# Moving the third pair's AV run behind the last score tile of a batch, in a fused attention and MLP kernel

## The chip, the cores and the metric

One core of one Trainium2 chip. The time is that of the whole program on the device in microseconds, as the median of several executions. A profiled execution also has a span, from the first to the last instruction, about 2 us shorter than the time, and a granted TensorE clock, 1.0 being full speed. A ratio of two kernels is the record's, made from their fast runs in the same rounds on the same chip; it isn't quite the ratio of the medians quoted beside it. All runs here count as fast but one of the kernel before (346.41 us at a clock of 0.985, beside e1 to e4), which the ratios leave out; where other runs had a slightly lower clock, that is said.

## The reference, cut to what matters

```python
scores = q @ k.T / 8 + (cum[:, None] - cum[None, :])   # cum: running sum of log f; causal
attn   = softmax(scores)
x      = attn @ v                   # 8 batches x 8 heads, 576 x 64
out    = gelu(x @ w_in) @ w_out     # 4608 x 512 -> 2048 -> 512
```

## The kernel before

Heads go in four pairs. A pair's scores are four tiles in PSUM, the memory that TensorE writes to, each of both heads: the two heads' matmuls contract over 64 rows and run side by side on the two halves of the array. ScalarE takes the exp of a tile, GpSimd masks the diagonal, and the AV run (the exps times v, 15 matmuls a head, contracting over all 128 rows) follows one pair later. VectorE divides by the row sums, a DMA transposes the result, and gemm1 reads it. Between the tiles stand steps of the previous batch's gemm2: "r" is a pair of half-array matmuls (contracting 64 rows each, into two banks that VectorE adds), "n" one full-array matmul. "r" steps go between scores because both use half-array mode.

```python
s_psum = tile_pool("s_psum", bufs=2)   # score tiles, two banks each   (abbreviated)
o_psum = tile_pool("o_psum", bufs=2)   # AV accumulators, one a head
m_psum = tile_pool("m_psum", bufs=2)   # gemm banks
...
PLAN = [                                # gemm2 steps of the previous batch
    (0, "o", 16 * "r"),
    (1, "m", 6 * "r" + "n" + 8 * "r" + "n"),
    (2, "m", 9 * "r" + "n" + 6 * "r"),
    (3, "s", 5 * "r" + 11 * "n"),
]
FILL = [[7, 6, 3, 3], [1, 3, 3, 2], [1, 3, 3, 3], [1, 3, 3, 3], [5]]
...
for i in range(HP):                     # 4 head pairs
    for t in range(4):
        scores(b, i, t)
        take(fill, counts[i][t])        # so many gemm2 steps
        if i and t == 1:
            av(i - 1)                   # AV and normalize of both heads
            x_dma(b, i - 1)
        ...
take(fill, counts[HP][0])
av(HP - 1)
x_dma(b, HP - 1)
take(fill, 4)
...
take(fill, 999)
# then gemm1 of this batch
```

Batch 0 and 1 have code of their own, which isn't changed. Batch 2 has its own lists, since it carries more gemm2 work; batches 3 to 7 use the lists above. In the profile L299 is a score matmul, L330 an AV matmul, L479 a gemm2 step, L385 gemm1, L309 the exp, L311 the mask, L343 and L344 the division, L487 and L490 the copy of one gemm2 bank and the addition of the other. PE stands for TensorE's matmuls, PEld for its weight loads, ACT for ScalarE, DVE for VectorE and POOL for GpSimd. A line of a timeline has start and length in us, engine, source line and operation, and in brackets the engine's idle time before it and what ended that.

The softmax here doesn't subtract the row's maximum and nothing guards it: scores larger than these inputs give would overflow.

## Time and profile before

| | before |
|---|---|
| median of 3 runs | 343.51 us (342.83 to 344.71) |
| profiled execution | 341.0 us, span 339.1 us, clock 0.998 |
| TensorE busy | 96% of the span, 90% of the chain that ended last |
| batch 3, 4 or 5, first score tile to the next batch's | 35.39 us |
| of it the fourth pair's first tile to the first gemm1 matmul | 8.69 us |
| the same stretch in batch 2 | 11.54 us |

The views behind this table are in the prediction, batch 2's with the result. The chain follows the work that ended last back, at each step to what it had waited for. The views are read as follows: TensorE is full, so only gaps in its stream and its own work can be won; a wait of another engine matters only where TensorE waits for it in turn.

### The profile page before, as it was taken

Reading aid. Unit: us, or ns where it says so; the run is one execution under the profiler, and the core shown is the slowest. Engines: PE = TensorE matmul, PEld = TensorE weight load, DVE = VectorE, ACT = ScalarE, POOL = GpSimd, SP = SyncE. Lnnn points to the kernel's source line nnn. Section 1 sums busy time; section 2 is a strip of 40 time slices with the busy share of each in tenths; the row PEclk is TensorE's granted clock in tenths of the full one; section 3 lists DMA queues with packets and bytes.
Section 4 is the critical chain, followed back from the end, with each engine's and each line's share of the span. In section 5 each row is a group of like instructions: output and inputs, shape, how many; then the busy total and the mean of one; then the engine's idle time right before and its main releaser. Section 6 shows DMA issues by size and latency. Waiting matters only on the chain.

```text
span 339.1 us, 7794 instructions
## 1 busy us (share of the span) xinstructions
PE 325.5 (96%) x3129; PEld 171.6 (51%) x3170; DVE 184.3 (54%) x417; ACT 209.9 (62%) x299; POOL 121.5 (36%) x250
## 2 busy tenths in 40 slices
PE   8799899999999999999999999999999999999995
PEld 4574455445554456445644565446544654444443
DVE  4770446664358935895579646974696541020011
ACT  6977786773735787378737873787368755404600
POOL 8190395037437053713453343624351420000000
PEclk9999999999999999999999999999999999999999
DMA  7999999979999799299959598589900241011013
GB/s 118 180 167 192 210 186 143 194 143 188 209 172 181 116 205 189 83 139 130 223 132 138 112 198 177 77 137 208 173 31 2 82 80 44 0 63 64 0 38 88
DMA packets 104628, 44.18 MB, mean 130 GB/s; under 512 B 83408, under 2 KB 100048, under 8 KB 104592
## 3 DMA queue, kind: packets, MB, share of 16 engines
q1 hardware_dynamic: 87296, 29.52, 45.4%
q0 software_dynamic: 16896, 13.63, 27.1%
q8 instruction: 25, 0.41, 0.5%
q10 hardware_dynamic: 400, 0.52, 0.4%
q14 instruction: 11, 0.09, 0.1%
HBM read 36.85 MB, written 9.44 MB: 137 GB/s over the span
## 4 chain that ended last, share of the span: by engine, by line
PE 90%; issue 2%; DMA 2%; ACT 2%; POOL 1%; DVE 1%; SPq 0%; POOLq 0%; DVEq 0%; ACTq 0%
PE ps L385 36%; PE ps L479 26%; PE o L330 10%; PE ps L421 8%; PE s L299 7%; DMA v_sb<-in_v_dram 2%; PE ps L517 2%; ACT e L309 1%; PE ps_x L363 1%; POOL q L107 1%; SPq L119 0%; POOL k L107 0%; PE ps_f L207 0%; DVE x L344 0%; DVE vw L268 0%
## 5 line engine op out<-in xcount | busy, mean ns | idle before, releaser
L405 ACT ACTIVATE g<-ps 128x512 bf16<-128x512 f32 x144 | 82.1, 601 | 80.3 <-PE ps L385 80.3
L309 ACT ACTIVATE e<-s 128x896 bf16<-128x896 f32 (+2 forms) x128 | 100.8, 834 | 26.6 <-PE s L299 24.5
L385 PE MATMUL ps<-xT,w_in_sb 128*128 128x512 bf16 x502 | 111.8, 379 | 0.5
L479 PE MATMUL ps<-w_out_sb,g 64*128 64x512 bf16 (+1 forms) x712 | 101.9, 376 | 0.8 <-issue 0.5
L385 PEld LDWEIGHTS <-w_in_sb 128*128 128x128 bf16 x576 | 55.9, 98 | 67.6 <-issue 1.8
L311 POOL TENSOR_SCALAR_AFFINE_SELECT e<-e 128x256 bf16<-128x256 bf16 (+1 forms) x135 | 49.1, 383 | 93.6 <-ACT e L309 93.3
L479 PEld LDWEIGHTS <-g 64*128 64x128 bf16 (+1 forms) x736 | 41.9, 94 | 39.8 <-issue 9.0
L299 PE MATMUL s<-qT,kT 64*128 64x320 bf16 (+4 forms) x384 | 45.6, 276 | 3.5 <-ACT e L309 2.3
L268 POOL TENSOR_TENSOR vw<-v_sb,wT 128x640 bf16<-128x640 f32 x30 | 38.6, 1289 | 24.9 <-PE s L299 14.5
L249 DVE COPY qT<-tq 64x288 bf16<-64x288 bf16 x96 | 42.2, 440 | 3.4 <-DMA tq<-q 2.0
L249 DVE COPY kT<-tk 64x288 bf16<-64x288 bf16 x96 | 40.7, 424 | 2.4 <-DMA tk<-k 0.8
L487 DVE COPY ot<-ps 128x512 f32<-128x512 f32 x25 | 17.3, 692 | 41.8 <-PE ps L479 41.8
L330 PE MATMUL o<-vw,e 128*128 128x65 bf16 x960 | 36.6, 194 | 3.0 <-issue 2.4
L330 PEld LDWEIGHTS <-e 128*128 128x128 bf16 x960 | 34.1, 98 | 6.8 <-POOL e L311 2.5
L344 DVE TENSOR_TENSOR x<-o,r 128x320 bf16<-128x320 f32 x64 | 31.5, 492 | 2.4 <-DMA xT<-x 0.2
L430 DVE COPY ot<-ps 128x512 f32<-128x512 f32 (+2 forms) x9 | 5.7, 632 | 48.9 <-PE ps L421 46.1
L299 PEld LDWEIGHTS <-kT 64*128 64x128 bf16 x384 | 19.7, 94 | 24.3 <-issue 11.7
L421 PE MATMUL ps<-w_out_sb,g 128*128 128x512 bf16 (+2 forms) x142 | 27.9, 355 | 0.1
L343 DVE RECIPROCAL r<-o 128x5 f32<-128x5 f32 x64 | 12.1, 190 | 22.9 <-PE o L330 22.7
L421 PEld LDWEIGHTS <-g 128*128 128x128 bf16 x144 | 13.5, 98 | 14.5
L490 DVE TENSOR_TENSOR ot<-ot,ps 128x512 f32<-128x512 f32 x25 | 17.2, 687 | 1.4
L385 PE MATMUL ps<-tails,w_in_sb 128*128 128x512 bf16 x62 | 14.2, 377 | 0.2
(67 smaller groups left out, 133.6 us busy)
## 6 DMA issues: line engine op xcount, KB each, us to landing
out_dram<-ot SPq DMA_DIRECT2D x32, 256.0 KB, 2.6
v_sb<-in_v_dram SPq DMA_DIRECT2D x24, 256.0 KB, 4.8
q<-in_q_dram POOLq DMA_DIRECT2D x6, 576.0 KB, 6.3
k<-in_k_dram POOLq DMA_DIRECT2D x6, 576.0 KB, 8.3
v_sb<-in_v_dram SPq DMA_DIRECT2D x22, 128.0 KB, 4.9
w_in_sb<-in_moe_w_in_dram POOLq DMA_DIRECT2D x4, 512.0 KB, 7.9
w_out_sb<-in_moe_w_out_dram POOLq DMA_DIRECT2D x4, 512.0 KB, 9.0
q<-in_q_dram POOLq DMA_DIRECT2D x4, 144.0 KB, 4.4
```

Of the source, the lines that this page charges most:

```text
L249: nc.vector.tensor_copy(rows[:, odd], src[odd * D : (odd + 1) * D, 2 * i + h].rearrange("d j p -> d p j"),)
L268: eng.tensor_tensor(vw(b)[:, hs, :, 0:D], v_sb[:, hs, :, :], w.unsqueeze(3).to_broadcast([P, 2, NBLK, D]), Alu.mult,)
L299: nc.tensor.matmul(to, *ab, start=half < 0, stop=half == 1 or not masked)
L309: nc.scalar.activation(et[:, :, z:c], st[:, :, z:c], Act.Exp, scale=scale)
L311: nc.gpsimd.affine_select(out=et[:, :, c0 + z : c0 + P], in_=et[:, :, c0 + z : c0 + P], compare_op=Alu.is_ge, fill=0.0, base=z, pattern=[[ ...
L330: nc.tensor.matmul(o[:, m, :], e_of[b, i, t][:, h, c : c + P], vw_of[b][:, 2 * i + h, n, :], start=(n == 0), stop=(n == m),)
L344: nc.vector.tensor_tensor(x_of[b, i][:, :, h, :], o[:, :, 0:D], r.unsqueeze(2).to_broadcast([P, NBLK, D]), Alu.mult,)
L385: nc.tensor.matmul(ps, w_in_sb[:, kt, ffb * P : (ffb + 1) * P], src[:, kt, 0:TC], start=(kt == 0), stop=(kt == n_dm - 1),)
L405: nc.scalar.activation(g_of[c][ffb], ps, Act.Gelu)
L421: nc.tensor.matmul(pss[ts][:, c0:c1], g_of[c][kt][:, ts * P : (ts + 1) * P], w_out_sb[:, kt, c0:c1], start=(kt == 0), stop=(kt == n_ff - 1),)
L479: nc.tensor.matmul(banks[r], g_of[c][kt][rows, ts * P : (ts + 1) * P], w_out_sb[rows, kt, :], start=kt == (steps.index("r") if r else 0), ...
L487: nc.vector.tensor_copy(ot, banks[1])
```

## The change

The intent: the third pair's AV run leaves its place between the fourth pair's second and third tile, where it costs a switch from half-array to full-array mode and one back, and goes behind the last tile, next to the fourth pair's AV run. Full-array gemm2 steps stand between the two runs and between the fourth pair's heads. The number of steps and the row blocks in which they are half- or full-array are fitted to that.

```diff
     PLAN = [ ...
-        (2, "m", 9 * "r" + "n" + 6 * "r"),
-        (3, "s", 5 * "r" + 11 * "n"),
+        (2, "m", 14 * "r" + 2 * "n"),
+        (3, "s", 16 * "n"),
     PLAN_1 = [ ...                        # batch 2
-        (2, "m", 12 * "r" + 4 * "n"),
+        (2, "m", 16 * "n"),
-    FILL = [[7, 6, 3, 3], [1, 3, 3, 2], [1, 3, 3, 3], [1, 3, 3, 3], [5]]
-    FILL_2 = [[8, 8, 8, 8], [8, 8, 4, 4], [4, 4, 4, 4], [4, 4, 4, 4], [4]]
+    FILL = [[7, 6, 3, 3], [1, 3, 3, 2], [1, 3, 3, 3], [2, 2, 2, 2]]
+    FILL_2 = [[8, 8, 8, 8], [8, 8, 4, 4], [4, 4, 4, 4], [6, 6, 5, 5]]
...
-        def av(i):
+        def av(i, n=0):
             for h in range(2):
                 attend(b, i, h, (0, 1, 2, 3, 4))
                 normalize(b, i, h)
+                if h == 0:
+                    take(fill, n)
+            x_dma(b, i)
...
-                if i and t == 1:
+                if i in (1, 2) and t == 1:
                     av(i - 1)
-                    x_dma(b, i - 1)
...
-        take(fill, counts[HP][0])
-        av(HP - 1)
-        x_dma(b, HP - 1)
+        av(HP - 2)
+        take(fill, 2)
+        av(HP - 1, 1)
         take(fill, 4)
```

## The prediction

> **What bounds the kernel now.** I read the busy table first: the share of the span in which TensorE has a matmul running, and the 40 slices, which show it near full from end to end at a granted clock of 1.0. Then the chain that ended last.
>
> ```profile
> PE 325.5 (96%) x3129; PEld 171.6 (51%) x3170; DVE 184.3 (54%) x417; ACT 209.9 (62%) x299; POOL 121.5 (36%) x250
> ...
> PE 90%; issue 2%; DMA 2%; ACT 2%; POOL 1%; DVE 1%; SPq 0%; POOLq 0%; DVEq 0%; ACTq 0%
> ```
>
> TensorE alone sets the time; 90% of the chain is its own work. So a change helps only by what it removes from TensorE's stream: work, switching gaps, or waits. Next I cut one steady batch (the one from 151.73 us) into scores of the first three head pairs, the fourth pair up to the first gemm1 matmul, and gemm1, with the view of busy time by window.
>
> ```profile
> 151.73:164.53 12.80, 12.47 (x169) 7.31 (x172) 7.94 (x21) 10.83 (x14) 4.83 (x14) 1.00 0.99 147
> 164.53:173.22 8.69, 8.48 (x114) 5.00 (x113) 3.94 (x10) 4.90 (x6) 3.90 (x9) 1.00 1.00 208
> 173.22:187.12 13.90, 13.85 (x64) 6.17 (x63) 13.29 (x26) 8.42 (x15) 6.47 (x9) 1.00 0.70 116
> ```
>
> Columns: length, then PE, PEld, DVE, ACT, POOL busy. A batch lasts 35.39 us. In the first stretch ACT is busy 10.83 of 12.80 us: behind TensorE it is a close second in the scores. The change leaves the order up to 164.53 alone, so the middle row is the one that it acts on. TensorE's timeline shows that stretch's skeleton (fourth pair's score tiles at 164.53, 165.07, 167.08 and 167.93; AV runs at 166.03 and 169.88; full-array gemm2 from 171.06):
>
> ```profile
> 165.07 0.37 PE L299 MATMUL s<-qT,kT 64*128 64x64 bf16 x4
> 165.23 0.64 PE L479 MATMUL ps<-w_out_sb,g 64*128 64x512 bf16 x4
> 166.03 1.12 PE L330 MATMUL o<-vw,e 128*128 128x65 bf16 x30 [0.16 <-issue]
> 167.08 0.36 PE L299 MATMUL s<-qT,kT 64*128 64x448 bf16 x2
> 167.28 0.81 PE L479 MATMUL ps<-w_out_sb,g 64*128 64x512 bf16 x6
> 167.93 0.30 PE L299 MATMUL s<-qT,kT 64*128 64x320 bf16 x2
> 168.06 1.89 PE L479 MATMUL ps<-w_out_sb,g 64*128 64x512 bf16 x16
> 169.88 1.12 PE L330 MATMUL o<-vw,e 128*128 128x65 bf16 x30
> ```
>
> 64*128 is a half-array matmul (two run side by side, one on each half of the rows), 128*128 a full-array one. And ACT's timeline of the same stretch:
>
> ```profile
> 163.37 1.65 ACT L309 ACTIVATE e<-s 128x896 bf16<-128x896 f32 x2 [0.93 <-PE s L299]
> 165.18 1.62 ACT L309 ACTIVATE e<-s 128x896 bf16<-128x896 f32 x2 [0.16 <-PE s L299]
> 167.54 1.51 ACT L309 ACTIVATE e<-s 128x896 bf16<-128x896 f32 x2 [0.75 <-PE s L299]
> ```
>
> The reader is to see that ACT is idle 0.93 and 0.75 us just after an AV run, and only 0.16 us otherwise: the AV run in the middle of a pair is the time in which the exps catch up.
>
> **What the Trainium skill says.** "TensorEngine Tiling (Array Packing)", Key Properties: changing the tiling mode, not just the tile, drains TensorE. The trace agrees and sizes it. A pair of half-array steps starts every 0.216 us (x16 in 1.89: seven spacings of 0.216 and a last matmul of 0.376). Before the AV at 169.88 the last half-array step started at 169.57, 0.31 earlier: 0.095 more than 0.216. The last AV matmul of the run at 166.03 starts at 166.95 and the scores at 167.08: 0.127, where AV matmuls follow each other at 0.031: 0.096 for the way back. So a switch costs 0.10 us either way. "ScalarE: Activation LUTs", What ACT_TABLE_LOAD costs, gives an ACTIVATE 0.833 ns an element and an overlap of some 93 ns between two; here 896 elements last 0.917 us and follow each other after 0.81, so it agrees, and the trace's values are used.
>
> **The change, part by part.** (a) In batches 3 to 7 the third pair's AV run leaves its place after the fourth pair's second tile and comes after the fourth tile, just before the fourth pair's AV. Before, the stretch has three switches (into AV, back to scores, into AV); after, one: two times 0.10 saved, 0.20 us a batch. The matmul work is equal: 26 gemm2 steps of 0.2155 (half- or full-array alike; the full ones at x10 in 2.32 give the same spacing), two AV runs of 0.95, 1600 score columns in 0.67: 8.2 us of the 8.69.
>
> (b) What the AV run hid comes out. Between the fourth pair's tiles there are now two steps each (0.43 us) and a tile of 0.13 to 0.19 us: about 0.6 a tile, while ACT needs 0.81, 0.71, 0.81, 0.60. Score PSUM has two buffers, so tile 2 waits for the exp of tile 0. Walk, on the half that runs later (0.17 behind, from an earlier wait): its first gemm2 step after tile 0 starts at 164.90, the second at 165.11, tile 1 at 165.33 (0.16), two steps, tile 2 due at 165.92. The exp of tile 0 starts at 165.18 in either kernel and ends 0.92 later, 166.09; a freed buffer is used 0.05 later (the exp that started at 159.37 ended at 160.28, the tile in its buffer started at 160.33): 166.14. Wait 0.22. Tile 3 is due 0.62 later, 166.76; the exp of tile 1 starts 0.81 after the first, 165.99, lasts 0.805: 166.79, and 0.05: 166.85. Wait 0.08. Tile 3 (0.13), two steps (0.43), a switch (0.10): AV of the third pair at 167.51.
>
> (c) The two AV runs are now 0.43 us apart, and the output accumulators have two buffers, one a head. The first head's AV ends about 168.15; VectorE, which has just copied a gemm2 bank (from 167.6, 0.69 us, the next operation 0.60 after its start), does the reciprocal at 168.21 and the scaling from 168.44 for 0.49 us; the buffer is free at 168.98. TensorE wants it at 167.51 + 0.95 + 0.43 = 168.89. Wait 0.10. The second head's buffer is free at about 169.61 and wanted at 168.99 + 0.47 + 0.22 = 169.68: the single step between the heads just covers it. Then 0.47 and 15 full-array steps (3.23): gemm1 starts at 173.38 instead of 173.22. So a batch becomes about 0.17 us longer: -0.20 for the switches, +0.22 +0.08 for ACT, +0.10 for VectorE, less some 0.03 that the old order lost otherwise. Five batches: +0.85.
>
> (d) Batch 2 has its own list. Its third gemm2 row block becomes full-array and begins after the fourth pair's second tile, so scores and full-array steps alternate: five switches where there were three, +0.20. Its first bank is the one that VectorE copies after the last half-array step (0.42 to the copy's start, 0.69, 0.05: free 1.16 after that step's start, wanted at 0.91): +0.25. And +0.05 for the accumulator as in (c). With five or six steps a tile ACT is not in the way. Sum +0.5.
>
> (e) Off the path: one VectorE addition of 0.69 us less a batch, and the transposing DMA of the third pair's output is issued some 2 us earlier or later without effect: the last one lands about 2.6 us after 171.5, and gemm1 asks for it 12 steps after 173.38, at 175.97.
>
> Total +1.35 us: 343.5 becomes 344.9. I lean slightly lower, as the walk counts each wait in full: 344.6.
>
> **Rivals.** First: only the switches count, ACT keeps up. Then five batches give -0.20 each and batch 2 stays within +0.5: 343.0. For it: the idle 0.93 and 0.75 of ACT, which look like slack. Against it: they lie after AV runs, and the waits of TensorE on the exps in the whole trace (2.3 us in 6) show that ACT is already the limit in spots without one. Second: the ACT wait is larger, as the exp of tile 0 may start later, or the masks on GpSimd (0.41 us each, after the exp) reach the fourth pair's AV too late; by the walk they end near 168.7 and are needed at about 169.15. A slip of 0.4 a batch would give 347. Third: the later DMA delays gemm1; its slack of some 1.9 us speaks against it; if it were lost and 0.5 more, the five batches would cost 2.5: 347.
>
> **Range and chances.** The walk's terms are each good to about 0.1 us, together about 0.25 a batch, so 1.3 over five, and the three runs before lie 1.9 apart. Low end 342.7 (the first rival and luck), high end 346.4. All rivals stay far inside 2% (6.9 us): faster 1%, within 2% 97%, slower 2%.
>
> **What would show it right or wrong.** Right: in the changed trace no AV run between the fourth pair's tiles; ACT without idle from that pair's first exp to its last; the third tile about 0.2 us after its two steps would let it start, with the exp named as releaser; the stretch to gemm1 8.85 us against 8.69; and in batch 2 a gap at the first full-array step of the third block. Wrong: ACT idle there, or the stretch at 8.5 or less, as the first rival has it; a wait on GpSimd before the last AV, or on a DMA in gemm1, for the others.

## The result, and the profile after

| | before | after |
|---|---|---|
| first comparison, 6 runs each | 343.17 us (342.60 to 344.71) | 342.92 us (342.66 to 343.23) |
| ratio | | 0.9987, 95% interval 0.9964 to 1.001 |
| span of the profiled execution | 339.1 us | 340.9 us |
| batch 3, 4 or 5 | 35.39 us | 35.74, 35.66, 35.66 us |
| batch 2 | 45.79 us | 46.39 us |

By the times the kernels are the same, with a ratio whose interval has 1 in it. By the two traces the changed kernel is 1.8 us longer, and every batch from 2 on is. (Of batch 3's 35.74 us, 0.09 are a wait for a DMA in gemm1; see (e) below.) The two readings don't fit, and the experiments below begin with that.

The view of busy time by window, after, with the same three stretches of the same batch as in the prediction (columns as there):

```profile
152.65:165.45 12.80, 12.79 (x171) 7.32 (x172) 7.17 (x18) 10.84 (x14) 4.85 (x14) 1.00 0.85 171
165.45:174.40 8.95, 8.88 (x110) 5.13 (x106) 3.65 (x10) 4.79 (x6) 3.91 (x9) 1.00 0.99 175
174.40:188.31 13.91, 13.91 (x66) 6.14 (x65) 13.29 (x28) 8.42 (x15) 6.52 (x9) 1.00 0.68 112
```

The scores of the first three pairs (12.80 us) and gemm1 (13.91 against 13.90) are what they were. The middle stretch, on which alone the change acts, went from 8.69 to 8.95 us. TensorE's timeline of it, after:

```profile
166.41 0.59 PE L479 MATMUL ps<-w_out_sb,g 64*128 64x512 bf16 x3
167.06 0.37 PE L299 MATMUL s<-qT,kT 64*128 64x448 bf16 x2
167.25 0.61 PE L479 MATMUL ps<-w_out_sb,g 64*128 64x512 bf16 x4
167.76 0.31 PE L299 MATMUL s<-qT,kT 64*128 64x320 bf16 x2
167.89 0.61 PE L479 MATMUL ps<-w_out_sb,g 64*128 64x512 bf16 x4
168.43 1.13 PE L330 MATMUL o<-vw,e 128*128 128x65 bf16 x30
169.40 0.59 PE L479 MATMUL ps<-w_out_sb,g 128*128 128x512 bf16 x2
170.00 0.63 PE L330 MATMUL o<-vw,e 128*128 128x65 bf16 x15
170.47 0.38 PE L479 MATMUL ps<-w_out_sb,g 128*128 128x512 bf16 x1
170.69 0.64 PE L330 MATMUL o<-vw,e 128*128 128x65 bf16 x15
```

No AV run stands between the score tiles any more. The third tile starts at 167.06, 1.61 us after the first at 165.45. ScalarE's timeline and one piece of the chain of waits say why:

```profile
166.09 3.02 ACT L309 ACTIVATE e<-s 128x896 bf16<-128x896 f32 x4 [0.16 <-PE s L299]
```

```profile
166.09 0.93 ACT e L309
```

The pair's four exps now run without any pause, where before there was one of 0.75 us after the second. The first of them ends at 167.01, and the third tile, which needs its buffer, starts 0.05 later. The chain of the kernel before has no exp in this stretch; this one runs through it. The second wait is in front of the fourth pair's AV run. Two full-array steps start at 169.40 and 169.61, so the run is due at 169.83; it starts at 170.00. All engines' timeline there, with VectorE's copy and reciprocal just ahead:

```profile
168.54 0.69 DVE L487 COPY ot<-ps 128x512 f32<-128x512 f32 x1 [3.15 <-PE ps L479]
169.15 0.18 DVE L343 RECIPROCAL r<-o 128x5 f32<-128x5 f32 x1
169.37 0.49 DVE L344 TENSOR_TENSOR x<-o,r 128x320 bf16<-128x320 f32 x1
```

```profile
169.97 0.22 PEld L330 LDWEIGHTS <-e 128*128 128x128 bf16 x5 [0.48 <-POOL e L311]
```

The scaling that frees the accumulator ends at 169.86. The weight load follows at 169.97 and the matmul at 170.00. The view names GpSimd's mask as the releaser of that load, but GpSimd's own timeline has its last mask from 169.18 for 0.41 us, so it was done by 169.59; VectorE came last.

In batch 2 the stretch went from 11.54 to 12.14 us. The same view, before and after:

```profile
90.89:102.43 11.54, 11.33 (x130) 6.20 (x129) 5.11 (x12) 4.74 (x6) 3.73 (x8) 1.00 1.06 180
```

```profile
90.86:103.00 12.14, 12.06 (x120) 6.11 (x117) 4.44 (x11) 4.74 (x6) 3.73 (x8) 1.00 1.03 193
```

and two pieces of the chain after, in which gemm2's third row block starts after a copy of VectorE:

```profile
92.56 0.70 DVE ot L487
...
93.30 1.02 PE ps L479 x4
```

### The profile page after: what moved, and what is told of

Same layout as the page of the kernel before. It is cut to its first block, busy times and chain, and to the rows that moved or that the text cites. A ratio compares the mean times of both kernels' runs of the same rounds, so it can differ in the third digit from the quotient of the medians.

```text
span 340.9 us, 7750 instructions
## 1 busy us (share of the span) xinstructions
PE 331.5 (97%) x3128; PEld 172.4 (51%) x3128; DVE 178.5 (52%) x411; ACT 209.5 (61%) x299; POOL 121.8 (36%) x250
## 4 chain that ended last, share of the span: by engine, by line
PE 90%; ACT 3%; DMA 2%; POOL 1%; issue 1%; DVE 1%; SPq 0%; ACTq 0%; POOLq 0%; DVEq 0%
PE ps L385 36%; PE ps L479 25%; PE o L330 9%; PE ps L421 8%; PE s L299 7%; ACT e L309 3%; DMA v_sb<-in_v_dram 2%; PE ps L517 2%; PE ps_x L363 1%; POOL q L107 1%; SPq L119 0%; POOL k L107 0%; PE ps_f L207 0%; DVE vw L268 0%; DVE qT L216 0%
## 5 line engine op out<-in xcount | busy, mean ns | idle before, releaser
L479 PE MATMUL ps<-w_out_sb,g 64*128 64x512 bf16 (+1 forms) x694 | 110.3, 377 | 0.1
L299 PE MATMUL s<-qT,kT 64*128 64x320 bf16 (+4 forms) x384 | 46.3, 276 | 3.3 <-ACT e L309 1.8
L249 DVE COPY kT<-tk 64x288 bf16<-64x288 bf16 x96 | 44.3, 461 | 5.0 <-DMA tk<-k 3.4
L249 DVE COPY qT<-tq 64x288 bf16<-64x288 bf16 x96 | 38.4, 400 | 1.7 <-DMA tq<-q 0.3
L330 PE MATMUL o<-vw,e 128*128 128x65 bf16 x960 | 37.7, 194 | 0.6 <-DVE vw L268 0.5
L487 DVE COPY ot<-ps 128x512 f32<-128x512 f32 x19 | 13.1, 692 | 47.1 <-PE ps L479 47.1
L299 PEld LDWEIGHTS <-kT 64*128 64x128 bf16 x384 | 21.3, 94 | 27.2 <-issue 14.6
L216 DVE COPY qT<-ps_f 128x576 bf16<-128x576 bf16 x7 | 5.3, 755 | 16.4 <-PE ps_f L207 16.4
```

The costliest lines, as they stand in the source:

```text
L249: nc.vector.tensor_copy(rows[:, odd], src[odd * D : (odd + 1) * D, 2 * i + h].rearrange("d j p -> d p j"),)
L299: nc.tensor.matmul(to, *ab, start=half < 0, stop=half == 1 or not masked)
L330: nc.tensor.matmul(o[:, m, :], e_of[b, i, t][:, h, c : c + P], vw_of[b][:, 2 * i + h, n, :], start=(n == 0), stop=(n == m),)
L479: nc.tensor.matmul(banks[r], g_of[c][kt][rows, ts * P : (ts + 1) * P], w_out_sb[rows, kt, :], start=kt == (steps.index("r") if r else 0), ...
L487: nc.vector.tensor_copy(ot, banks[1])
```

## The experiments

The theory going in: the trace is right. In batches 3 to 7 the change saves two switches and pays with waits for exps and for accumulators; in batch 2 it adds switches and waits. Rivals: the profile of before was a lucky execution and the change is neutral or a gain; or the gaps next to mode changes are not the cost of the switch. Twelve runs of ten kernels were made, on three chips; all gave correct results. By the 2% verdict every one of them is "same"; the argument is about smaller differences. The table has what they gave; "scores to gemm1" is a batch's first score tile to its first gemm1 matmul, in batches 3 to 5 (21.48 us before).

| run | ratio to before | 95% interval | span | scores to gemm1 | batch 2, the same |
|---|---|---|---|---|---|
| e1_before_again | 0.9987 | 0.9959 to 1.0014 | 339.1 | 21.47 to 21.48 | 31.88 |
| e5_after_again | 1.0053 | 1.0032 to 1.0075 | 341.0 | 21.75 to 21.76 | 32.48 |
| e11_after_third | 1.0029 | 1.0004 to 1.0053 | 341.6 | 21.74 to 21.75 | 32.48 |
| e2_late_b3to7 | 1.0025 | 1.0005 to 1.0046 | 340.5 | 21.74 to 21.75 | 31.88 |
| e3_late_b2 | 1.0025 | 1.0002 to 1.0048 | 339.8 | 21.48 | 32.48 |
| e4_more_steps | 1.0070 | 1.0047 to 1.0093 | 342.6 | 21.66 to 21.67 | 32.48 |
| e6_split_run | 1.0015 | 0.9996 to 1.0033 | 342.4 | 21.72 to 21.73 | 31.88 |
| e7_three_between | 1.0011 | 0.9986 to 1.0035 | 339.9 | 21.58 | 32.33 |
| e8_balanced | 0.9939 | 0.9916 to 0.9963 | 338.2 | 21.26 to 21.27 | 31.88 |
| e12_balanced_again | 0.9960 | 0.9944 to 0.9977 | 339.0 | 21.26 to 21.27 | 31.88 |
| e10_balanced_kt | 0.9953 | 0.9923 to 0.9984 | 338.3 | 21.26 to 21.27 | 31.88 |
| e9_all_late | 1.0084 | 1.0050 to 1.0118 | 342.2 | 21.44 to 21.45 | 31.88 |

The last two columns repeat to 0.02 us from execution to execution, while the spans of one kernel differ by 1 us and more. So the columns carry the argument on single parts, and the ratios carry the verdict on the whole. Batch 6 is left out of the column because the old order takes 21.60 us there, in both of its profiles; the cause wasn't looked for, and the change costs 0.15 us in that batch.

**e1_before_again: the kernel before, unchanged.**

> The kernel before, once more, unchanged. Theory A (the profile before was a lucky execution): its profile had a span of 339.1 us and 341.0 us measured, while its timed runs lay at 342.6 to 344.7; if the typical execution is slower, the new profile shows a span of 340.5 us or more, and its runs scatter by 1 us or more. Theory B (the first profile was typical): span 339.1 us again. The ratio to the kernel before must be 1.000 within 0.003 either way.

The profile again has a span of 339.1 us, and every batch from 2 on repeats within 0.01 us of the first profile. Theory A as it was put (a lucky profile) falls, though the runs do scatter by 3.5 us. Most of that goes with the clock. Beside this kernel and the three that were sent with it, the kernel before ran 61 times: 43 executions with a granted clock of 0.998 or more had a median span of 339.3 us, 17 with 0.990 to 0.995 lay at 340.4 to 343.1, and the slow one at 344.4.

**e5_after_again and e11_after_third: the changed kernel, twice more, without an edit.**

> The changed kernel again, on one chip with the kernel before, with the clock of every run. Theory A (the traces are typical; the six runs of before beside the first measurement were executions in which the clock dipped for one or two windows of 3.4 us): in executions with a granted clock of 0.998 or more, spans near 340.9 us against 339.2 for before, and a ratio of about 1.005. Theory B (on the chip the change is neutral or a gain, as the first ratio of 0.9987 says): spans equal within 0.5 us at equal clock.

> The changed kernel a third time. The first comparison gave 0.9987 (six runs each), the second 1.0053. If the first was an accident of six disturbed executions of the kernel before, the ratio is again 1.003 to 1.008 and, among executions with a granted clock of 0.998 or more, the changed kernel's median span is 1.5 to 2.5 us above that of before. If it depends on the chip, a ratio near 1.000 may come back.

Both intervals lie above 1. Among executions with a clock of 0.998 or more the median spans were 341.8 (13 runs) against 339.4 (34 runs of before) on one chip, and 341.4 (17) against 339.35 (26) on another: 2.4 and 2.05 us, somewhat more than the 1.8 of the first two profiles. The spread of the changed kernel has a second cause besides the clock: the profile of e11 starts batch 2 at 71.20 us where the first one had 70.52, so 0.7 us of its span are from batches 0 and 1, which the change doesn't touch.

Why, then, 0.9987 in the first comparison? All six runs of before took 342.6 us or more there. On the other chips, of the 172 fast runs of before that stood beside other kernels, 60 took as long, and 48 of these had a clock under 0.998. The clocks of those six runs aren't recorded, so that they were disturbed in that way is likely but not shown. With six against six runs that comparison couldn't tell.

**e2_late_b3to7 and e3_late_b2: one part of the change alone.** The first keeps batch 2 as before, the second batches 3 to 7. The core of e2:

```diff
-        (2, "m", 16 * "n"),                     # PLAN_1
+        (2, "m", 12 * "r" + 4 * "n"),
-                if i in (1, 2) and t == 1:
+                if i in ((1, 2, 3) if b == 2 else (1, 2)) and t == 1:
-        av(HP - 2); take(fill, 2); av(HP - 1, 1)
+        if b == 2: take(fill, 4); av(HP - 1)
+        else:      av(HP - 2); take(fill, 2); av(HP - 1, 1)
```

e3 is its mirror image, with the old lists for batches 3 to 7.

> The change in batches 3 to 7 alone, batch 2 as before. The traces before and after differ by 0.27 us in each of those batches, against the new order, and by 0.6 us in batch 2. My theory (a switch pair saved 0.20, exp waits and the accumulator wait cost 0.45): span 340.4 us, that is 0.6 us below the changed kernel's 340.9 and 1.3 above the first profile before. Rival (the order itself is a gain and the first profile was luck): span at or below 339.5 us.

> The change in batch 2 alone. My theory: 0.6 us more than the kernel before in the same state (batch 2's stretch from the fourth pair's first tile to gemm1 12.1 us against 11.5). Rival: batch 2 unchanged within 0.1 us.

Both as the theory had it: 0.27 us more in each of batches 3 to 5, 0.60 us more in batch 2, and each part leaves the other's batches alone. Neither part is a gain.

**e6_split_run: the cost of switches by themselves.** The old order, with the third pair's AV run cut in two by one half-array step that was taken from a place a little later.

```diff
                 normalize(b, i, h)
+                if b > 2 and i == 2 and h == 0:
+                    take(fill, 1)
...
-                take(fill, counts[i][t])
+                take(fill, counts[i][t] - (b > 2 and (i, t) == (3, 2)))
```

> The kernel before, with the third pair's AV run split in batches 3 to 7 by one half-array gemm2 step between its two heads (taken from the steps after the fourth pair's third tile): the same work, two more switches a batch. If a switch costs 0.10 us, 10 switches add 1.0 us: span 340.1 us. If switches cost nothing by themselves (rival: the gaps were waits for masks or exps), span 339.1 within 0.3.

```profile
166.40 0.64 PE L330 MATMUL o<-vw,e 128*128 128x65 bf16 x15
166.97 0.39 PE L479 MATMUL ps<-w_out_sb,g 64*128 64x512 bf16 x2
167.29 0.65 PE L330 MATMUL o<-vw,e 128*128 128x65 bf16 x15
```

The first head's run would be followed after 0.47 us; the half-array step comes after 0.57. It would be followed after 0.216; the second head comes after 0.32. So two switches cost 0.20 us by these gaps. The batch is 35.63 instead of 35.39 us, 0.24 more with the same work; about 0.04 of that lies between the fourth tile and the fourth pair's AV run (1.99 us against 1.95), and its cause wasn't looked for. The profiled execution's span of 342.4 us is from elsewhere: batches 2 to 6 end where they should (batch 7 starts at 259.13, 1.1 after the kernel before), 2.0 us more than in the kernel before come after the last matmul, and the median span of 21 runs at full clock was 340.5.

**e4_more_steps: more steps between the fourth pair's tiles.**

```diff
-    FILL = [..., [1, 3, 3, 3], [2, 2, 2, 2]]
+    FILL = [..., [1, 3, 3, 3], [3, 3, 2, 2]]
```

> The changed kernel with gemm2 steps 3, 3, 2, 2 between the fourth pair's score tiles instead of 2, 2, 2, 2, two full-array steps fewer at the batch's end; everything else equal. My theory: tile 2's wait of 0.22 us and tile 3's of 0.08 for the exps vanish, so each of the five batches gets 0.3 us shorter: span about 339.4 us. Rival (the waits are not on the exps but move along): span within 0.3 us of 340.9.

A miss, and an instructive one. The wait on the exps did go: from the first tile to the third pair's AV run it is 3.11 us with ten steps on the way, against 2.98 with eight; two steps are 0.43 us of work, so 0.30 of waiting was filled. But the third row block of gemm2 now ends before the AV runs, and its copy and its addition stand on VectorE ahead of the division, as VectorE's timeline shows:

```profile
168.84 0.69 DVE L487 COPY ot<-ps 128x512 f32<-128x512 f32 x1 [2.69 <-PE ps L479]
169.63 0.69 DVE L490 TENSOR_TENSOR ot<-ot,ps 128x512 f32<-128x512 f32 x1
170.24 0.19 DVE L343 RECIPROCAL r<-o 128x5 f32<-128x5 f32 x1
```

From one AV run to the other it takes 1.79 us instead of 1.57, so 0.22 of the 0.30 went back into the accumulator wait: 21.67 against 21.75. On top, batches 3 and 6 were 36.21 and 36.83 us long, 0.6 and 1.3 more than 35.58, because gemm1 waited for the third pair's transposing DMA. The chain in batch 3:

```profile
136.04 4.28 DMA xT<-x
```

Its landing took 4.28 us; the median of these DMAs in the kernel before is 2.8. Issued later, as here, it has less room for that.

**e7_three_between: a third full-array step in front of the fourth pair's AV run.**

```diff
-        take(fill, 2)
+        take(fill, 3)
```

> The changed kernel with three full-array steps instead of two between the third and fourth pair's AV runs (one fewer at the end), in all six batches. The trace shows 0.17 to 0.2 us of wait for the scaling of the first head there. If that wait is a fixed moment, one step of 0.2155 us covers it: 6 times 0.17 to 0.2, so about 1.1 us less, span 339.8 us. Rival (VectorE's work moves along, or the wait is only a matter of the load of weights): under 0.4 us less.

```profile
169.10 0.81 PE L479 MATMUL ps<-w_out_sb,g 128*128 128x512 bf16 x3
169.75 0.64 PE L330 MATMUL o<-vw,e 128*128 128x65 bf16 x15
```

Three steps take 0.65 us, and the AV run starts right then. The batches became 0.17 us shorter, batch 2 0.15: the accumulator wait was a fixed moment and one step covers it.

**e8_balanced and e12_balanced_again: the late run with both waits taken away, in batches 3 to 7.** Built on e2, so batch 2 is as before.

```diff
-    FILL = [..., [1, 3, 3, 3], [2, 2, 2, 2]]
+    FILL = [..., [1, 3, 3, 3], [3, 3, 2, 0]]
-            take(fill, 2)
+            take(fill, 3)
```

> Late third pair in batches 3 to 7 with both of its waits taken away: half-array steps 3, 3, 2, 0 around the fourth pair's tiles (so the exps keep up and no step follows the last tile) and three full-array steps between the two AV runs; batch 2 as before. By my terms the stretch from the fourth pair's first tile to gemm1 becomes 8.36 us, against 8.69 before and 8.95 in the changed kernel, so 0.33 us a batch under the kernel before: span 337.5 us, ratio 0.995. Rival (a third wait follows, on the masks or on VectorE): stretch 8.6 or more. Rival (the third pair's transposing DMA, issued late, is now asked for too soon): single batches 0.5 to 1.5 us longer in gemm1.

> The balanced version again, on the same chip as the changed kernel: ratio to the kernel before 0.992 to 0.997, and 3 us under the changed kernel.

```profile
164.70:173.17 8.47, 8.47 (x110) 5.38 (x106) 3.75 (x10) 4.89 (x6) 3.90 (x9) 1.00 1.02 183
```

TensorE is busy in all of the 8.47 us, and the chain there holds nothing but its work. That is 0.11 above the forecast, but it is what the change's 8.95 less the 0.30 of e4 and the 0.17 of e7 comes to, 8.48: the waits measured one by one add up. It is 0.22 under the kernel before (8.69), which is what one pair of switches costs in e6. The kernel before is beaten in both comparisons, 0.9939 and 0.9960. On the chip where the changed kernel ran too (e11), the median was 340.41 us against 343.35 for the change and 341.78 for before. Part of the first ratio is the clock: all 11 runs of e8 had 0.998 or more, and 5 of the 20 runs of before beside it had less. Among runs with 0.998 or more the median spans are 1.5 us (e8) and 1.05 us (e12) under before, where five batches of 0.21 make 1.05.

**e10_balanced_kt: gemm1's start reordered on top of e8.**

```diff
-        for ffb in range(2):
-            gemm1(b, ffb, (2,), pss[ffb])
-        pss += [gemm1(b, ffb, (0, 1, 2), spare()) for ffb in (2, 3)]
+        pss += [gemm1(b, ffb, (0, 1), spare()) for ffb in (2, 3)]
+        for ffb in range(4):
+            gemm1(b, ffb, (2,), pss[ffb])
```

> The kernel of e8_balanced with gemm1's first matmuls reordered in batches 2 to 7: the first two contraction blocks of four output blocks, then the third block of all four, then the fourth; the third pair's transposed output is asked for 0.86 us later, the fourth's at the same time. If the late DMA is what scatters, the single long batches vanish and the span is at or below e8's, about 337.5 us; if DMA is no matter, equal to e8 within 0.2.

Nothing: batches of 35.17 to 35.18 us in both. In these traces e8 has no DMA wait that a later use could remove, so whether a later use would help where there is one stays untested.

**e9_all_late: all four AV runs at the end.** PLAN's row blocks became 16 "r", 16 "r", 14 "r" and 2 "n", 16 "n"; the third of them takes its banks from the AV accumulators' pool, the pool of the divided results has four buffers instead of three, batch 2 keeps the old order, and, against the changed kernel:

```diff
-    FILL = [[7, 6, 3, 3], [1, 3, 3, 2], [1, 3, 3, 3], [2, 2, 2, 2]]
+    FILL = [[7, 6, 3, 2], [3, 3, 3, 2], [3, 3, 3, 2], [3, 2, 1, 0]]
-            av(HP - 2); take(fill, 2); av(HP - 1, 1)
+            take(fill, 5)
+            for i in range(HP): av(i, 1)      # a step after each head
```

> All four AV runs of batches 3 to 7 at the end, one full-array step after each head, half-array steps spread as 7,6,3,2 / 3,3,3,2 / 3,3,3,2 / 3,2,1,0 so that each tile is just due when the exp two tiles earlier ends; batch 2 as before. By my terms: six of seven switches a batch fall away (0.6 us), and the waits of the old order on exps and gemm2 banks with them (0.3 to 0.4): about 1.0 us a batch, span about 334 us, ratio 0.985. Rival: exps or VectorE are behind anyway and the time comes back as waits: span 338 or more. Rival: the four transposing DMAs bunch and gemm1 waits for them.

Wrong by 8 us. Both rivals came true. The six switches are gone, yet the stretch is 21.45 us, hardly under 21.48: the chain runs through the exps tile after tile, and of the eight heads in a row the first of each pair waits for the scaling that frees its accumulator: a pair each 1.54 us (167.71, 169.25, 170.79, 172.33), where its matmuls and steps alone are 1.37. And the transposing DMAs bunch: batch 3's four are issued within 4.5 us. Its gemm1, and the same of batch 4 for comparison:

```profile
137.72:153.34 15.62, 14.06 (x65) 6.12 (x64) 14.89 (x33) 8.42 (x15) 7.03 (x11) 1.00 0.67 105
...
174.79:188.78 13.99, 13.99 (x65) 6.17 (x65) 13.34 (x28) 8.42 (x15) 6.93 (x11) 1.00 0.72 119
```

with 1.6 us in which TensorE waits; the chain there holds

```profile
135.83 4.43 DMA xT<-x
```

Removing switches pays only as long as the engines that the AV run gave time to can still follow.

**The clock, seen once.** The profiled execution of e12 happened to have a clock of 0.995. In the others TensorE has half its clock, if at all, only after its last matmul (from 337.63 us against 335.34 in the kernel before), so a clock of 0.998 there is no loss. e12's view by window:

```profile
40.16:43.57 3.41, 2.25 (x53) 1.49 (x48) 3.10 (x6) 3.35 (x6) 3.40 (x6) 1.00 1.18 216
43.57:46.98 3.41, 3.41 (x39) 2.14 (x38) 1.89 (x5) 2.34 (x4) 2.43 (x6) 0.50 1.19 192
```

For 3.41 us TensorE ran at half its clock, right after a window of that length in which it was busy 2.25 us of 3.41. This is in batch 1, in code that is the same in all these kernels. "TensorE: Matmul & The Clock Gate", Part 1, describes a free-running activity window of 3413 ns after which the clock is halved or restored; the length agrees. How little work it takes for that isn't shown: in e8 the same stretch looks alike and the clock stays full, and where the windows begin isn't known there.

```profile
40.16:43.57 3.41, 2.30 (x58) 1.64 (x55) 2.96 (x5) 3.34 (x7) 3.12 (x4) 1.00 1.15 224
43.57:46.98 3.41, 3.31 (x50) 1.88 (x49) 2.09 (x6) 3.13 (x4) 3.40 (x9) 1.00 1.14 187
```

So such an execution says nothing about the change. That all low-clock executions lose time in this place isn't shown: only this one was seen with its trace.

## Why the prediction was right or wrong

The median, 342.92 us, lies in the range 342.7 to 346.4, and the verdict "within 2%" is right. The lean to the slower side isn't confirmed by the first comparison, which can't tell the kernels apart, but is by the next two, with 1.0053 and 1.0029 against the forecast's 1.003 (344.6 over 343.5). The absolute 344.6 was too high in all three, by 1.7, 0.8 (e5, 343.77) and 1.25 us (e11, 343.35). That the first median lies in the range owes something to luck: it is 0.2 us above a low end that was set for the first rival, and by that number alone the rival's 343.0 was the better forecast. What bears the walk out is the traces, step by step:

- **(a) Switches, 0.20 us a batch.** Right: e6 gives 0.20 for a pair by its gaps and 0.24 by its batch, and e8, with one switch where before had three, saves 0.22.
- **(b) Exps.** Right, to the hundredth. From the fourth pair's first tile the walk put the third tile at 1.61 us (166.14 less 164.53), the fourth at 2.32 and the AV run at 2.98; the trace has 1.61, 2.31 and 2.98. e4 filled 0.30 us of waiting with work, as the walk's 0.22 and 0.08 had it.
- **(c) Accumulators.** Right mechanism, the term mis-sized: 0.10 forecast, 0.17 in the trace and in e7. The walk let TensorE start 0.05 us after the scaling ends. The trace has 0.14: the weight load in front of the matmul came only 0.11 after the scaling's end, in e7 too. The stretch to gemm1 was forecast at 8.85 us and is 8.95; a batch costs 0.27 more, not 0.17.
- **(d) Batch 2.** 0.60 against 0.5; e3 shows it alone. Its accumulator term was the small one again, 0.15 (e7) against 0.05. The bank's wait can be read in the trace: full-array steps start at 92.61, 92.84 and 93.30, and the last gap is 0.46 instead of 0.216, so it is 0.25 us, as forecast. What is left, 0.20, is the forecast for the added switches; no run measures them alone.
- **(e) Off the path.** Nearly right for the change itself: in two of its profiles one gemm1 lost 0.09 us, in batch 3 of the first to the second pair's DMA (landing 4.61 us), which the change doesn't move, and in batch 6 of e11 to the third pair's (4.80 us). But the slack is smaller than the walk made it. It worked out that of the fourth pair's DMA; the third pair's is asked for after four matmuls, and with a landing of 2.72 us in batch 4 it has 1.65 us. e4 and e9, which issue the DMAs later still, lost up to 1.7 us in single batches, because landings don't always take 2.6 us: in these two traces the third pair's took up to 4.54.
- **Sum.** +1.35 us forecast, +1.8 between the two profiles. The missing half microsecond is mostly (c), five times 0.1 us. The 2.4 and 2.05 us between the full-clock medians of e5 and e11 are more than either; e11's profile puts 0.7 of its span into batches 0 and 1, and the rest stays open.
- **Rivals.** The first (only the switches count) is refuted by e2, and by the exps without a pause. The second didn't occur; the third cost the change 0.09 us in one batch of e11, and cost e4 and e9 more.

The forecast took 343.51 us as a firm base. That median was of three runs in which 341.0 had also been seen, by the profile; that span should have warned that the runs before were not all of one kind. In the later rounds the kernel before had medians of 341.66 to 342.15 us.

## What to carry to other kernels

A run of other work in the middle of a bound engine's stream is not only a cost of two mode switches: it may be the time in which the engines behind it catch up, so look at what is idle right after it before moving it. If it is moved, give its time back in the places that had lived on it: here moving steps between the tiles, and one more step in front of the accumulators, turned a loss of 0.27 us a batch into a gain of 0.21. For differences of half a per cent, compare only executions with the same granted clock, and single parts by the length of the stretch that they change.

## What the Trainium skill lacked or had wrong

- "TensorEngine Tiling (Array Packing)", Key Properties, says that a change of mode drains TensorE, without a size. In this kernel it is 0.10 us by the gaps; e6 adds two of them a batch, and the batch gets 0.24 us longer.
- "TensorE: Matmul & The Clock Gate", Part 1, gives idle time of TensorE as the cause of half clock, a whole window or many short pauses, but not how busy a window has to be. Here the clock was halved for 3.41 us after a window of that length in which the trace has TensorE busy for 2.25 us (e12), and not after the same stretch with 2.30 us (e8).
- The same page's specifications say that weight loads are pulled ahead of matmuls in flight, and nothing of a matmul that waits for a buffer. In front of the fourth pair's AV run the load wasn't early: the scaling that freed the accumulator ended at 169.86, the load came at 169.97 and the matmul at 170.00. In front of the third score tile a load stands at 166.46, and the matmul came at 167.06, 0.05 us after the exp that freed its buffer.
- No page that I read gives the scatter of transposing DMAs from SBUF to SBUF: a median of 2.8 us from issue to landing in the kernel before, and up to 5.76 us (e12, batch 3) in these traces.
